# An attention, mixture-of-experts and FFN kernel: other places for sums, gates' steps and transposes, and a shifted buffer

## The chip, the cores and the metric

The kernel runs on one core of one Trainium2 chip. The metric is the time of one execution on the device, in microseconds (us). Before the change the median of three runs is 2119.26 us (2117.87 to 2119.72).

## The reference, cut to what matters

Three layers follow one another on 2304 tokens (4 x 576):

```python
# 1. attention with random features, 4 batches x 8 heads x 576 x 64, 128 features
q_p, k_p = phi(q_s), phi(k_s)               # exp(x @ omega.T - |x|^2/2 - max) / sqrt(m)
num = q_p @ (k_p.T @ v);  den = q_p @ k_p.sum(tokens) + 1e-6
x = (num / den)                             # -> [2304, 512]
# 2. eight experts, all of them for all tokens, D = 512, F = 1024
P = np.exp(x @ w_gate - max)
for _ in range(8):                          # the gates
    P /= P.sum(1, keepdims=True) + 1e-9
    P /= P.sum(0, keepdims=True) + 1e-9
    P *= N / E
out = sum(P[:, e:e+1] * (np.maximum(x @ w1[e], 0) @ w2[e]) for e in range(8))
# 3. FFN, d_ff = 2048
h = out @ w_in
return (h * sigmoid(1.702 * h)) @ w_out
```

## The kernel before

**Numbers in two parts.** Products on TensorE (PE) are made of three: an operand is split in a high part, rounded to `fp32r` by a cast on ACT, and a low part, the difference, made on DVE or POOL (`split`, L577). So a tile `w` gives `g0h`, `g0l` and so on, `x` gives `xh` and `xl`, and hh is followed by hl.

**Tiles.** The tokens lie in three blocks `j` of six tiles of 128. A weight chunk has 256 columns of `d_ff`: four chunks for each expert, eight for the FFN, which the code counts as expert 8 (`E`). A *visit* is one chunk on one block. It has an `up` part (x times w1, tiles `ph`) and a `down` part (h times w2, tiles `py`, 36 matmuls of 512 columns in 18 or 36 steps, `down`, L890 to L917), whose results are added into `acc` (`add_up`).

**Order of visits.** Expert 0's visits run between the pieces of the attention (half blocks, as soon as their x is there), the last of them behind it. Then come experts 1 to 7 and the FFN. In all these later visits but the FFN's first chunk, `up_fast` (L803 to L888) takes the place of `up`: seven products of six matmuls (le, ri, pc, le, ri, le, pd, L822) in place of eight, three of which have as their operand not x but sums of its quarters, the tiles `th` and `tl`. These sums are made once per block and layer, on POOL, DVE and ACT (`x_sums` L744, `x_sum4` L780, with the helpers `pool_tt` L735 and `dve_tt` L739). The first fast visit starts at 409.9 us.

**What sets the order.** The order is that in which the code is written: generators give work in pieces, and each `yield` gives the planned length of the PE work just issued (0.68 us for three `py`, 2.08 for twelve `ph`, 1.04 for a product of `up_fast`). At each yield the driver (L1113) makes one step of `background()` (L975), which issues the next sum of x, and at every third yield one step of `gates`. Every engine does its own instructions in the order of issue.

- `urgent` holds the sums of x in two lanes, `spare` the FFN's weights. `background()` issues from `urgent` whenever something is there; a fast visit that needs sums not yet issued takes them by `hurry`.
- `split1` (L631) splits a chunk's w1: three casts on ACT, then g0l, g1l and g2l on POOL. It is called in `down` of the visit before.
- `sinkhorn` (L478 to L521) makes the gates in turns of two steps. Step A is five DVE instructions (r, r, rr, lg, cs, L496 to L503). Step B is the PE product `pc` of ones and cs (L508) and three DVE instructions (ct, rc, lg, L511 to L513). There are eight turns.
- `ffn_in` (L1007) turns the FFN's x: for each tile four PE transposes (`xt`, L342), then the copy to yh and the difference yl. It runs beside the `down` parts of three visits about the end of expert 7; `late` holds subtractions that are put off.
- In `down`, `outer` chooses the order of the loops over the two halves `f` of w2 and the three tiles `t`: with `outer` f is the outer loop.

```python
        outer = cur.fast and e == E and not final          # L896
            if cnt % 3 == 2:                               # L1115
                next(gates, None)
            background()
```

Of the kernel before, what the change touches and what calls it, by code (L numbers as in the profile page):

```python
# [10 lines left out]
F32 = mybir.dt.float32  # L11
# [9 lines left out]
def tile_performer_sinkhorn_moe(  # L21
# [23 lines left out]
    E, _, F = w1.shape  # L45
    F2 = w_in.shape[1]
    P = 128
# [13 lines left out]
    ST = 6  # L61
    NB = NTILE // ST
# [5 lines left out]
    sm = ctx.enter_context(tc.tile_pool(name="sm", bufs=1))  # L68
# [21 lines left out]
    now = [0.0]  # L90
# [17 lines left out]
    def ps(name):  # L108
        return pp.tile([P, 512], F32, tag="ps", bufs=6, name=name)
# [13 lines left out]
    om_lo = ph["sb"].tile([P, 2 * M], F32R, name="om_lo")  # L123
    wg_raw = ph["sb"].tile([P, NK, E], F32, name="wg_raw")
    wg = ph["sb"].tile([P, NK, 2 * E], F32R, name="wg")
    lg = cst.tile([P, NTILE, E], F32, name="lg")
    pg = lg

# [59 lines left out]
    late = []  # L188

    def run_late():  # L190
        while late:
            late.pop(0)()
# [144 lines left out]
    def transpose_x(x, t, dst_h, dst_l):  # L337

        c = slice(t * P, (t + 1) * P)
        pt = ps("xt")  # L340
        for kk in range(NK):
            nc.tensor.transpose(pt[:, kk * P : (kk + 1) * P], x[:, kk * P : (kk + 1) * P], ident)  # L342
        pv = pt.rearrange("p (k n) -> p k n", k=NK)
        nc.scalar.copy(dst_h[:, :, c], pv)
        late.append(
            lambda: nc.vector.tensor_tensor(
                out=dst_l[:, :, c], in0=pv, in1=dst_h[:, :, c].bitcast(F32), op=ALU.subtract
            )
        )
# [301 lines left out]
    acc = {}  # L651
# [75 lines left out]
    sums_done = set()  # L727
# [162 lines left out]
    def down(cur, j, h, halves, first, final):  # L890

        e, _ = cur.ch
        if (e // E, j) not in accs:
            accs.add((e // E, j))
            acc[j] = new_acc(j, "a" if e < E else "o")
        outer = cur.fast and e == E and not final  # L896
        for th in halves:
            py = {}
            halves = range(NF) if th == 0 else range(NF - 1, -1, -1)
            tiles = range(3 * th, 3 * th + 3)  # L900
            todo = [(f, t) for f in halves for t in tiles] if outer else [(f, t) for t in tiles for f in halves]
            for f, t in todo:
                if t not in py:
                    py[t] = ps("py")
                c = slice(t % 3 * P, (t % 3 + 1) * P)
                hh, hl = h[th, f]
                w2h, w2l = cur.w2[f]
                for m, (a, w) in enumerate(((hh, w2h), (hh, w2l), (hl, w2h))):
                    nc.tensor.matmul(  # L909
                        py[t], a[:, c], w,  # L910
                        start=f == halves[0] and m == 0, stop=f == halves[1] and m == 2,
                    )
                if f == halves[1]:
                    add_up(cur, j, t, py[t], first, final)
                    if t > tiles[0]:
                        run_late()
                yield 3 * 0.2275  # L917
# [37 lines left out]
    n_exp = len(visits)  # L955
# [9 lines left out]
    urgent = [deque(), deque()]  # L965
    spare = deque()

    def run(q):
        if next(q[0], "end") == "end":
            q.popleft()  # L970
# [4 lines left out]
    def background():  # L975

        if begun():
            run(spare)
        elif any(urgent):
            for lane in urgent:  # L980
                if lane:
                    run(lane)
        elif spare and may_start[0]:
            run(spare)

    def hurry(q):

        force[0] = True
        run(spare if begun() else q)
        force[0] = False  # L990
# [3 lines left out]
            hurry(q)  # L994

    may_start = [False]

    def apply_gate(j):

        for _ in gates:  # L1000
            pass
        for t in range(ST):
            yield
            o = acc[j][:, t, :]
            nc.scalar.activation(o, o, AF.Copy, scale=pg[:, ST * j + t, 0:1])

    def ffn_in(j):  # L1007

        nblk[j] = hi, lo = new_block("y")
        for t in range(ST):  # L1010
            yield
            transpose_x(acc[j][:, t, :], t, hi, lo)
            yield
            run_late()

    nblk = {}

    def moe():

        cn = v = 0  # L1020
        for idx, (ch, j, halves) in enumerate(visits):
            if idx:
                new = ch != visits[idx - 1][0]
                cn, v = (cn + 1, 0) if new else (cn, v + 1)
            cur, nx, n2 = (chunks[cn + i] if cn + i < len(chunks) else None for i in range(3))
            left = 1
            while idx + left < len(visits) and visits[idx + left][0] == ch:
                left += 1
            while idx < n_first and not ready.issuperset((j, th) for th in halves):
                yield None  # L1030
            may_start[0] = cur.fast and ch[0] < E and left > 1
            if idx == n_exp - NB - 1:
                settle(spare)
            if n_exp <= idx < n_exp + NB:
                blk_h[j], blk_l[j] = nblk[j]

            def prep(at, cur=cur, v=v):
                if at == "w2" and v == 0:
                    if cur.fast:
                        cur.split2(len(cur.w2))  # L1040
                    else:
                        cur.split2(0)
                        cur.split2(1)

            key = (ch[0] // E, j)
            if cur.fast:
                for kk, lane in enumerate(urgent):
                    while (key, kk) not in sums_done:
                        hurry(lane)
                h = yield from up_fast(cur, j, prep)  # L1050
            else:
                h = yield from up(cur, j, halves, prep)
            if v == 0 and nx:
                nx.load2()
            if nx and left <= 2:
                nx.make_sums()
            side = None
            if n_exp - 2 <= idx <= n_exp:
                side = ffn_in(idx - n_exp + 2)
            elif n_first - 1 <= idx < n_first + 2:  # L1060
                side = apply_gate(idx - n_first + 1)
            first = (key, halves[0]) not in seen
            seen.update((key, th) for th in halves)
            for n, dt in enumerate(down(cur, j, h, halves, first, ch == chunks[-1].ch)):
                if n == 2 * len(halves) - 1 and left == 1 and nx:
                    for i in range(3):
                        nx.split1(i, nc.gpsimd)
                    if n2:
                        n2.load1()
                if side and (n > 4 or idx != n_first - 1):  # L1070
                    next(side, None)
                yield dt
            for _ in side or ():
                pass
            if idx == n_first - 1 or ch == (E, 0):
                sum_up(x_sum4(key, blk_h[j], blk_l[j]))
            if n_exp - 2 <= idx <= n_exp:
                i = idx - n_exp + 2
                sum_up(x_sums((1, i), *nblk[i]))

    with tc.manual_schedule():
        setup()
        load_tile("k", 0, NT)
        for what, t in (("v", 0), ("v", 1), ("q", 0), ("v", 2), ("q", 1), ("v", 3), ("v", NT), ("q", 2), ("q", 3)):
            load_tile(what, 0, t)
        load_gate()
        chunks[0].load1()
        chunks[0].load2()
        m = moe()
        credit = 0.0  # L1090
        for i, dt in enumerate(attention()):
            if i == 14:
                setup_gate()
            if i == 22:
                for g in range(3):
                    chunks[0].split1(g, nc.gpsimd)
                chunks[1].load1()
            credit += dt
            while credit > 0:
                got = next(m)  # L1100
                if got is None:
                    credit = 0.0
                else:
                    credit -= got
        enter_phase("exp")
        ready.update((j, th) for j in range(NB) for th in range(2))
        spare.extend(double_pieces())
        for j in range(NB):
            sum_up(x_sums((0, j), blk_h[j], blk_l[j]))
            if j < 2:  # L1110
                sum_up(x_sum4((0, j), blk_h[j], blk_l[j]))
        pool[0] = now[0]
        for cnt, dt in enumerate(m):  # L1113
            now[0] += dt
            if cnt % 3 == 2:  # L1115
                next(gates, None)
            background()
        phase.close()
# [30 lines left out]
```

## Time and profile before

| | us |
|---|---|
| median of three runs | 2119.26 |
| profiled execution, its own time | 2119.29 |
| its span in the trace | 2116.0 |
| PE busy | 2086.4 (99%) |
| DVE, ACT, POOL busy | 1419.0, 797.3, 500.7 |
| mean granted clock of the PE | 0.996 |

The span is 3.3 us shorter than the time of the execution it belongs to. PE is busy nearly always, by the table of busy time; since a matmul's end is modelled there, a wait is better read from the start times of the timeline, and a clock of less than 1 from the table of stretches (1 is 2.4 GHz, the lower level is 1.2 GHz). A row of a timeline has in brackets how long the engine sat idle before it and what released it.

### The profile page before, as it was taken

What the parts mean: (1) busy time and instruction counts of PE and PEld (TensorE: products, weight loads), DVE (VectorE), ACT (ScalarE), POOL (GpSimd) and SP (SyncE); (2) the same over time, 40 slices, a digit from 0 to 9 for tenths busy, and PEclk for the clock granted to TensorE, in tenths of its full rate; (3) what the DMA queues carried; (4) which work ended last, traced back from release to release, by engine and by line L of the source; (5) the groups of instructions that cost most, each with busy time, mean ns of one, the idle gap of its engine ahead of it and who ended that gap; (6) DMA issues with size and microseconds to landing.
All of it is one profiled execution on the core that took longest, in us unless ns stands there. A gap on an engine that the chain in (4) does not pass through costs nothing.

```text
span 2116.0 us, 29301 instructions
## 1 busy us (share of the span) xinstructions
PE 2086.4 (99%) x11040; PEld 1891.9 (89%) x11040; DVE 1419.0 (67%) x2630; ACT 797.3 (38%) x1770; POOL 500.7 (24%) x517
## 2 busy tenths in 40 slices
PE   8999998999999999999999999999999999999999
PEld 8999987899899998999989999899899988989987
DVE  7666546866767667676666676665555586676666
ACT  7655543433223232232333323223333255443443
POOL 3222225712212211121122111211211048111120
PEclk9999999999999999999999999999999999999999
DMA  8333211211111111111112111110010000000002
GB/s 164 89 81 90 70 41 40 65 43 43 50 45 43 51 60 43 50 50 43 46 43 58 53 50 43 51 38 21 22 39 21 20 21 21 21 21 21 21 21 90
DMA packets 147965, 100.54 MB, mean 48 GB/s; under 512 B 63600, under 2 KB 125040, under 8 KB 147824
## 3 DMA queue, kind: packets, MB, share of 16 engines
q1 hardware_dynamic: 147824, 98.68, 16.8%
q8 instruction: 86, 1.41, 0.3%
q14 instruction: 55, 0.45, 0.1%
HBM read 85.54 MB, written 13.11 MB: 47 GB/s over the span
## 4 chain that ended last, share of the span: by engine, by line
PE 94%; DVE 3%; ACT 2%; issue 0%; POOL 0%; DMA 0%; SPq 0%; ACTq 0%; POOLq 0%; DVEq 0%
PE py L909 45%; PE le L822 15%; PE ri L822 10%; PE ph L713 6%; PE pc L822 5%; PE pd L822 5%; PE num L304 2%; PE kv L274 1%; PE xt L342 1%; PE pt L215 1%; PE qt L297 1%; PE pj L240 1%; PE pj L242 1%; PE pj L241 1%; DVE mx L244 1%
## 5 line engine op out<-in xcount | busy, mean ns | idle before, releaser
L909 PE MATMUL py<-w,hh 128*128 128x512 f32 x2880 | 896.9, 392 | 1.8 <-ACT hh L676 1.8
L909 PEld LDWEIGHTS py<-w,hh 128*128 128x128 f32 x2880 | 534.0, 188 | 106.4 <-ACT hh L676 3.5
L909 PE MATMUL py<-w,hl 128*128 128x512 f32 x1440 | 564.2, 392 | 0.0
L926 DVE SCALAR_TENSOR_TENSOR a<-py,lg,a 128x512 f32<-128x512 f32 x504 | 367.1, 746 | 136.7 <-PE py L909 136.3
L909 PEld LDWEIGHTS py<-w,hl 128*128 128x128 f32 x1440 | 270.5, 188 | 59.1 <-DVE hl L684 1.7
L579 POOL TENSOR_TENSOR g0l<-w,g0h 128x768 fp32r<-128x768 f32 (+1 forms) x52 | 87.1, 1675 | 724.8 <-ACT g0h L578 706.2
L840 ACT COPY m<-le 128x384 f32<-128x384 f32 x105 | 50.3, 479 | 540.3 <-PE le L822 540.3
L563 POOL TENSOR_TENSOR tmp<-tmp 128x256 f32<-128x256 f32 x64 | 47.3, 738 | 637.3 <-DVE tmp L560 347.4
L833 DVE TENSOR_TENSOR pc<-pc,m 128x384 f32<-128x384 f32 x105 | 59.5, 566 | 147.1 <-PE pc L822 147.1
L628 POOL TENSOR_TENSOR w<-w 128x256 f32<-128x256 f32 x140 | 109.6, 804 | 44.8 <-DMA w<-scr_in 22.3
L579 DVE TENSOR_TENSOR w<-r,w 128x512 fp32r<-128x512 f32 x104 | 78.8, 771 | 52.3 <-ACT w L578 52.2
L578 ACT CAST w<-r 128x512 fp32r<-128x512 f32 x104 | 63.6, 629 | 116.1 <-PE py L909 115.5
L686 DVE SCALAR_TENSOR_TENSOR hl<-pc,hh 128x384 fp32r<-128x384 f32 x84 | 46.8, 557 | 90.1 <-ACT hh L678 88.4
L854 ACT COPY u<-le 128x384 f32<-128x384 f32 x105 | 50.5, 481 | 135.4 <-PE le L822 135.4
L260 ACT ACTIVATE feat<-pj,nb 128x128 f32<-128x128 f32 x272 | 74.0, 386 | 68.6 <-DVE nb L256 65.1
L930 DVE TENSOR_TENSOR o<-py,o 128x512 f32<-128x512 f32 x126 | 84.0, 685 | 21.7 <-PE py L909 21.7
L833 DVE TENSOR_TENSOR le<-le,m 128x384 f32<-128x384 f32 x105 | 59.3, 565 | 45.7 <-ACT m L874 45.7
L678 ACT ACTIVATE hh<-ri 128x384 fp32r<-128x384 f32 x84 | 41.2, 491 | 92.2 <-DVE ri L833 92.2
L822 PE MATMUL le<-th,g1h 128*128 128x384 f32 x210 | 71.5, 340 | 1.0 <-ACT m L840 1.0
L822 PE MATMUL le<-th,g2h 128*128 128x384 f32 x210 | 71.5, 340 | 0.9 <-ACT u L854 0.9
L874 ACT COPY m<-pd 128x384 f32<-128x384 f32 x105 | 49.9, 475 | 57.3 <-PE pd L822 57.2
L822 PE MATMUL ri<-th,g0h 128*128 128x384 f32 x210 | 71.4, 340 | 0.0
(253 smaller groups left out, 4599.8 us busy)
## 6 DMA issues: line engine op xcount, KB each, us to landing
w<-in_moe_w_dram SPq DMA_DIRECT2D x176, 128.0 KB, 2.3
r<-in_moe_w_dram SPq DMA_DIRECT2D x44, 512.0 KB, 3.7
raw<-in_moe_w_in_dram SPq DMA_DIRECT2D x32, 256.0 KB, 3.0
raw<-in_moe_w_out_dram SPq DMA_DIRECT2D x32, 256.0 KB, 3.0
k<-in_k_dram SPq DMA_DIRECT2D x16, 256.0 KB, 4.0
v<-in_v_dram SPq DMA_DIRECT2D x16, 256.0 KB, 4.8
q<-in_q_dram SPq DMA_DIRECT2D x16, 256.0 KB, 4.6
scr_in<-tmp SPq DMA_DIRECT2D x32, 128.0 KB, 1.9
```

What stands on the lines that cost most here:

```text
L260: nc.scalar.activation(f[:, h, :], pvs[h // 4][:, h % 4, :], AF.Exp, bias=nb[:, h : h + 1])
L578: nc.scalar.copy(hi, r)
L579: eng.tensor_tensor(out=lo, in0=r, in1=hi.bitcast(F32), op=ALU.subtract)
L628: nc.gpsimd.tensor_tensor(out=r[:, o], in0=r[:, x], in1=r[:, y], op=ALU.subtract)
L713: nc.tensor.matmul(o, w[kk][a], x[j][:, 2 * kh + kk, th * Q : (th + 1) * Q], start=m == 0, stop=m == 3 * NK - 1,)
L822: nc.tensor.matmul(o, a[kk][x], b[kk][y], start=start and kk == 0 and n == 0, stop=kk == 1 and n == 2, skip_group_check=True,)
L833: nc.vector.tensor_tensor(out=o, in0=a, in1=b, op=ALU.add)
L840: nc.scalar.copy(m1, le)
L854: nc.scalar.copy(u2, le)
L909: nc.tensor.matmul(py[t], a[:, c], w, start=f == halves[0] and m == 0, stop=f == halves[1] and m == 2,)
L926: nc.vector.scalar_tensor_tensor(out=o, in0=py, scalar=pg[:, n, e : e + 1], in1=o, op0=ALU.mult, op1=ALU.add)
L930: nc.vector.tensor_tensor(out=o, in0=py, in1=o, op=ALU.add)
```

## The change

1. A tile `pad` of 32 bytes per partition is put in the pool that lies ahead of others in the on-chip memory. `th` and `tl`, which began 32 bytes past a multiple of 64, begin on a multiple of 64; so do the tiles om_hi and om_lo of the attention. Some others (feat, ft, some of the temporaries) begin at 32 past it instead; x, h and the weights stay on 64.
2. While a `down` part of expert 0 runs behind the attention, `background()` issues no sum of x (if none of `spare` is begun), up to the point where the next chunk's splits are issued.
3. `gates` makes a step when 2.7 us of planned time have gone by since the last one, instead of at every third yield.
4. `ffn_in` issues the transposes of three tiles together, the first three tiles in the `up` part of the visit, the others in `down`.
5. In the FFN's last chunk `outer` holds too, but for the last half block.

```diff
+    sm.tile([P, 8], F32, name="pad")
...
-        outer = cur.fast and e == E and not final
         for th in halves:
+            outer = cur.fast and e == E and not (final and th == 1 and j == NB - 1)
...
         if begun():
             run(spare)
+        elif any(urgent) and paused[0]:
+            return
         elif any(urgent):
...
-        for t in range(ST):
-            yield
-            transpose_x(acc[j][:, t, :], t, hi, lo)
-            yield
-            run_late()
+        for g in range(0, ST, 3):
+            for t in range(g, g + 3):
+                transpose_x(acc[j][:, t, :], t, hi, lo)
+            for _ in range(3):
+                yield
+                if late:
+                    late.pop(0)()
+            for _ in range(3):
+                yield
...
+                if side and n > 0 and idx >= n_exp - 2:
+                    next(side, None)
...
+            paused[0] = ch[0] == 0
             for n, dt in enumerate(down(cur, j, h, halves, first, ch == chunks[-1].ch)):
                 if n == 2 * len(halves) - 1 and left == 1 and nx:
                     for i in range(3):
                         nx.split1(i, nc.gpsimd)
                     if n2:
                         n2.load1()
+                    paused[0] = False
...
+        gate_at = now[0]
         for cnt, dt in enumerate(m):
             now[0] += dt
-            if cnt % 3 == 2:
+            if now[0] > gate_at:
+                gate_at = now[0] + 2.7
                 next(gates, None)
```

Each engine has the same instructions as before; where they stand is shown at three places. Line numbers from 124 on are one higher in the changed kernel, and more further down.

**POOL, where the attention has ended** (one chunk of expert 0 gives way to the next at 311 to 320 us; u and t are temporaries of the sums, xh and xl the first block's x). Before:

```order
L735 TENSOR_TENSOR u<-xh,t 128x384
L735 TENSOR_TENSOR u<-u,xl 128x384
L735 TENSOR_TENSOR u<-xh,t 128x384
L735 TENSOR_TENSOR u<-u,xl 128x384
L579 TENSOR_TENSOR g0l<-w,g0h 128x2x256
L579 TENSOR_TENSOR g1l<-w,g1h 128x256
L579 TENSOR_TENSOR g2l<-w,g2h 128x256
```

After:

```order
L580 TENSOR_TENSOR g0l<-w,g0h 128x2x256
L580 TENSOR_TENSOR g1l<-w,g1h 128x256
L580 TENSOR_TENSOR g2l<-w,g2h 128x256
L736 TENSOR_TENSOR u<-xh,t 128x384
L736 TENSOR_TENSOR u<-u,xl 128x384
L736 TENSOR_TENSOR u<-xh,t 128x384
L736 TENSOR_TENSOR u<-u,xl 128x384
```

The three splits have come ahead of the first four sums.

**DVE, the third turn of the gates** (the end of step B of the second turn, step A, step B; tl is a sum of x, hl a low part of h). Before:

```order
L512 RECIPROCAL rc<-ct 128x8
L513 SCALAR_TENSOR_TENSOR lg<-lg,rc 128x144
L496 TENSOR_REDUCE r<-lg 128x18
L497 TENSOR_SCALAR r<-r 128x18
L498 RECIPROCAL rr<-r 128x18
L499 TENSOR_TENSOR lg<-lg,rr 128x144
L503 TENSOR_REDUCE cs<-lg 128x8
L511 TENSOR_SCALAR ct<-pc 128x8
L512 RECIPROCAL rc<-ct 128x8
L513 SCALAR_TENSOR_TENSOR lg<-lg,rc 128x144
L739 TENSOR_TENSOR xl<-u,xh 128x384
L739 TENSOR_TENSOR t<-xh,xl 128x384
```

After:

```order
L513 RECIPROCAL rc<-ct 128x8
L514 SCALAR_TENSOR_TENSOR lg<-lg,rc 128x144
L687 SCALAR_TENSOR_TENSOR hl<-ph,hh 128x384
L497 TENSOR_REDUCE r<-lg 128x18
L498 TENSOR_SCALAR r<-r 128x18
L499 RECIPROCAL rr<-r 128x18
L500 TENSOR_TENSOR lg<-lg,rr 128x144
L504 TENSOR_REDUCE cs<-lg 128x8
L740 TENSOR_TENSOR tl_3887<-u,th_3886 128x384 x2
L512 TENSOR_SCALAR ct<-pc 128x8
L513 RECIPROCAL rc<-ct 128x8
L514 SCALAR_TENSOR_TENSOR lg<-lg,rc 128x144
```

Step B of the third turn follows step A directly before; now there are two sums and, on PE, more matmuls between them.

**PE, the end of the last-but-one visit of expert 7's last chunk** (a is the first block's sum over the experts, turned for the FFN). Before:

```order
L822 MATMUL pd<-xl,g2h 128x384
L909 MATMUL py<-w_16288,hh 128x512
L909 MATMUL py<-w_16289,hh 128x512
L909 MATMUL py<-w_16288,hl 128x512
L909 MATMUL py<-w_16300,hh 128x512
L909 MATMUL py<-w_16301,hh 128x512
L909 MATMUL py<-w_16300,hl 128x512
L342 MATMUL xt<-ident,a_1111 128x128 x4
L909 MATMUL py<-w_16288,hh 128x512
```

After:

```order
L823 MATMUL pd<-xl,g2h 128x384
L910 MATMUL py<-w_16289,hh 128x512
L910 MATMUL py<-w_16290,hh 128x512
L910 MATMUL py<-w_16289,hl 128x512
L343 MATMUL xt<-ident,a_1112 128x128 x12
L910 MATMUL py<-w_16301,hh 128x512
L910 MATMUL py<-w_16302,hh 128x512
L910 MATMUL py<-w_16301,hl 128x512
```

Four transposes behind every six `py` have become twelve at a time; the other twelve of this block stand in the `up` part ahead, behind its second product.

## Rows read from the trace of the kernel before

**Rows 1.** the page's chain that ended last, shares of the span by engine

```profile
PE 94%; DVE 3%; ACT 2%; issue 0%; POOL 0%; DMA 0%; SPq 0%; ACTq 0%; POOLq 0%; DVEq 0%
```

**Rows 2.** stretches: length, busy us (xcount) PE, PEld, DVE, ACT, POOL, clock, DMA

```profile
313.00:327.00 14.00, 9.12 (x35) 8.14 (x33) 5.29 (x7) 1.86 (x4) 6.57 (x7) 0.76 0.25 77
342.00:354.00 12.00, 9.63 (x38) 7.64 (x37) 10.97 (x21) 4.66 (x10) 9.70 (x10) 0.86 0.00 0
```

**Rows 3.** waits, 300 to 426 us: engine, line, releaser; total us, times, longest

```profile
PE pc L508 <- DVE cs L503: 7.9, 4, 2.4
PE ph L713 <- POOL g2l L579: 4.9, 1, 4.9
PE le L822 <- ACT m L840: 1.0, 1, 1.0
```

**Rows 4.** timeline: start, us, engine, line, op, tiles [idle before]

```profile
311.44 0.41 ACT L578 CAST g2h<-w 128x256 fp32r<-128x256 f32 x1
...
311.86 1.26 POOL L735 TENSOR_TENSOR u<-xh,t 128x384 f32<-128x384 f32 x1 [10.99 <-DVE t L739]
...
319.79 0.69 PE L713 MATMUL ph<-xh,g2l 128*128 128x384 f32 x1 [4.88 <-POOL g2l L579]
...
325.96 0.34 PE L713 MATMUL ph<-xl,g0h 128*128 128x384 f32 x1
```

**Rows 5.** timeline of POOL near 370 us: one split by itself

```profile
370.30 0.73 POOL L579 TENSOR_TENSOR g2l<-w,g2h 128x256 fp32r<-128x256 f32 x1
```

**Rows 6.** timeline of DVE: first and last instruction of two steps A

```profile
347.22 0.30 DVE L496 TENSOR_REDUCE r<-lg 128x18 f32<-128x144 f32 x1
349.31 0.41 DVE L503 TENSOR_REDUCE cs<-lg 128x8 f32<-128x144 f32 x1
...
370.43 0.29 DVE L496 TENSOR_REDUCE r<-lg 128x18 f32<-128x144 f32 x1
371.74 0.43 DVE L503 TENSOR_REDUCE cs<-lg 128x8 f32<-128x144 f32 x1
```

**Rows 7.** groups by forms (busy, mean ns), then PE's timeline of a visit

```profile
L822 PE MATMUL le<-th,g1h 128*128 128x384 f32 x210 | 71.5, 340 | 1.0 <-ACT m L840 1.0
L822 PE MATMUL le<-xh,g0h 128*128 128x384 f32 x168 | 57.1, 340 | 0.0
L822 PE MATMUL pc<-xh,g0h 128*128 128x384 f32 x168 | 56.4, 336 | 0.0
...
1800.93 0.34 PE L822 MATMUL le<-th,g1h 128*128 128x384 f32 x1
...
1801.99 0.34 PE L822 MATMUL ri<-yh,g1h 128*128 128x384 f32 x1
...
1803.04 0.34 PE L822 MATMUL le<-th,g2h 128*128 128x384 f32 x1
...
1804.10 0.34 PE L822 MATMUL pd<-yh,g2h 128*128 128x384 f32 x1
...
1805.14 0.63 PE L909 MATMUL py<-w,hh 128*128 128x512 f32 x2
...
1813.34 0.33 PE L822 MATMUL le<-yh,g0h 128*128 128x384 f32 x1
```

**Rows 8.** timeline of PE and POOL where the FFN begins

```profile
1715.46 0.63 PE L909 MATMUL py<-w,hh 128*128 128x512 f32 x2
...
1725.44 1.29 POOL L579 TENSOR_TENSOR g0l<-w,g0h 128x512 fp32r<-128x512 f32 x1
...
1726.42 0.42 PE L713 MATMUL ph<-yh,g0h 128*128 128x384 f32 x1
```

**Rows 9.** POOL's tile u (min/median/max ns), and the end of expert 1's splits

```profile
L735 POOL TENSOR_TENSOR u<-u,xl x18: 992/1015/1347, 313.2 to 419.5; 128x384 f32<-128x384 f32 x18
...
411.58 1.62 POOL L579 TENSOR_TENSOR g2l<-w,g2h 128x512 fp32r<-128x512 f32 x1
```

**Rows 10.** timeline of PE in the last chunk, the first block

```profile
2071.17 0.73 PE L909 MATMUL py<-w,hh 128*128 128x512 f32 x2 [0.20 <-ACT hh L676]
```

More of the change, by code (lines that the diff above doesn't have):

```diff
@@ L996, in tile_performer_sinkhorn_moe @@
     may_start = [False]
+    paused = [False]
     def apply_gate(j):
@@ L1045, in moe @@
             key = (ch[0] // E, j)
[L1046 to L1056, printed above, removed]
             side = None
@@ L1061, in moe @@
                 side = apply_gate(idx - n_first + 1)
+            if cur.fast:
+                for kk, lane in enumerate(urgent):
+                    while (key, kk) not in sums_done:
+                        hurry(lane)
+                todo = up_fast(cur, j, prep)
+            else:
+                todo = up(cur, j, halves, prep)
+            n = 0
+            while True:
+                try:
+                    dt = next(todo)
+                except StopIteration as end:
+                    h = end.value
+                    break
+                if side and n > 0 and idx >= n_exp - 2:
+                    next(side, None)
+                n += 1
+                yield dt
+            if v == 0 and nx:
+                nx.load2()
+            if nx and left <= 2:
+                nx.make_sums()
             first = (key, halves[0]) not in seen
             seen.update((key, th) for th in halves)
+            paused[0] = ch[0] == 0
             for n, dt in enumerate(down(cur, j, h, halves, first, ch == chunks[-1].ch)):
```

## The prediction

> **What bounds the kernel now.** I read the page first: the chain that ended last runs through TensorE (PE) for 94% of the span [rows 1], so the time is the PE's own stream plus the moments in which it waits or runs at half its clock. Then the table of stretches, to see where those moments are: between 313 and 354 us the granted clock falls to 0.76 and 0.86 while PE is busy for only 9 to 10 us out of 12 to 14 [rows 2]. The table of waits from 300 to 426 us names the causes: one wait for the last weight split of expert 0 on POOL, four waits of `pc` for the gates' column sums on DVE, one for a copy on ACT [rows 3]. The timelines then give each wait its place. Everything ahead of 250 us and from 426 to 1710 us is a PE stream without such holes; there only the length of a matmul itself could change.
>
> The changed kernel issues the same instructions on every engine in another order, so the sum is made of waits that go or come, of half clock behind them, and of matmuls that may get shorter. It is made against the profiled execution's 2119.29 us, which is the median of the runs (2119.26) to 0.03 us; the 3.3 us around the span stay.
>
> **1. Weight splits ahead of the sums.** The three casts that feed the splits are over at 311.85, but POOL has just begun four sums (u at 311.86, about 1.1 us each), and the splits come behind them; PE, which had asked at about 314.9, gets g2l only at 319.79 and has waited 4.88 [rows 4]. In the new order (shown with the change) the splits stand ahead of those four sums. Alone, the three take 1.29 + 0.73 + 0.73 = 2.75 us [rows 5, 8], since g1l has g2l's shape; begun behind the first cast, two casts of 0.4 earlier at about 311.1, they are done between 313.9 and PE's asking at 314.9. Gain 4.9, bounds 4.0 (splits stretched as beside DVE work) and 5.3.
>
> Behind that wait the PE ran at half its clock: from 319.79 to 325.96 it started 19 matmuls in 6.17 us [rows 4], where a group of six takes 1.05 at full clock [rows 7], so 19 take 3.33. Lost: 2.8, which goes with the wait; 0 if something else still lets the clock fall there.
>
> **2. Gates' steps by time.** The four waits of `pc` cost 7.9 us on the PE's row [rows 3], 8.5 with the matmuls that restart behind them. Each step A (five DVE instructions, from r to cs) is followed by step B, whose `pc` needs cs. Before, B follows A by three yields, which are three pieces of 0.68 us (2.05) wherever both fall in `down`; now by at least 2.7 by the kernel's own count, so at least 0.68 more for each of the four: 2.7. Step A itself takes 2.09 + 0.4 = 2.5 beside POOL's sums and 1.31 + 0.4 = 1.7 with POOL at rest [rows 6], and POOL's sums now pause in each `down` of expert 0 until the splits are out: up to 0.8 more each, 3.1. Gain between 2.7 and 5.8; I take the middle, 4.3, since the pause covers part of those stretches only; the outer bound is all 8.5. What stays is hidden by nothing: the PE waits in order, with all later `py` behind it. The wait at 347 to 350 us was followed by a clock of 0.86 over 12 us [rows 2], 12 x 0.14 = 1.7 lost. I count 1.7, bounds 0 and 1.7.
>
> **3. The sums that are put off.** The PE's 1.0 us wait for a copy in the first fast visit [rows 3] lies beside a crowded ACT, POOL and DVE; with the gates' end shifted I take that gain as 1.2. In exchange about 22 sums of x and four weight sums (3.5) stand behind expert 1's splits, which end at 413.2 [rows 9]. A fast visit takes 7 x 1.05 + 8.2 = 15.6 [rows 7]; the last product on sums in expert 1's third visit comes 2 x 15.6 + 5 x 1.05 = 36.4 behind the start of its first (409.9), and 33 of these are left when the splits end. At 1.02 each (median) they need 22 x 1.02 + 3.5 = 25.9, at 1.35 each (the longest) 33.2 [rows 9]; with the ACT casts and DVE subtractions between them that comes near what is there. Cost 0.8, bounds 0 and 4.5 (1.35 each, and about 4 us of chained casts that POOL waits for). Net gain 0.4, bounds +1.2 and -3.3.
>
> **4. Transposes in two groups.** Now six groups of four stand between the `py` of one block: 1715.46 to 1726.42, 10.96 us, where 36 `py` alone take 8.20 (1805.14 to 1813.34) [rows 7, 8]. That is 0.46 per group of four, nearly all of it the four transposes' own time, which stays; fewer turns give 0 to 0.3. But half of each block's transposes leave for `up`, so the PE comes to (E,0)'s first `ph` at 8.20 + 3 x 0.46 = 9.6 us behind its first `py`, while POOL, with sums of the FFN's x ahead of it, ends g0l at 1725.44 + 1.29 - 1715.46 = 11.3 [rows 8]. The second matmul of `ph` needs g0l: a new wait of 1.4 (PE asks 0.3 later), bounds 0.2 (if the sums move up with the transposes that feed them) and 2.5, with 1.7 of half clock behind it at worst. The pause doesn't help here, it holds for expert 0 alone. Net -1.1 (slower), taken as +1.4 less 0.3.
>
> **5. Last chunk by w2 halves.** In the last chunk the second `py` pair of each block waits 0.20 for the second half of h, and that pair takes 0.73 [rows 10] where 0.63 is usual [rows 7]: 0.3 for each of three blocks, 0.9. In the new order the first half's matmuls of three tiles come first, 2.0 us of cover rather than 0.68. A tile's output then closes later, but the last half block keeps its order. Bounds 0 and 1.7.
>
> **6. Sums of x on 64 bytes.** The new tile of 32 bytes moves th and tl from 32 past a multiple of 64 bytes onto it. In one visit, two groups of six matmuls on th take 1.06 each (1800.93, 1803.04) and the two behind them on yh take 1.05 and 1.04 [rows 7]: 0.015 a group. Three groups in each of 105 visits (210 matmuls of each form, two in a visit) make 315 x 0.015 = 4.7. By the durations alone, 340 against 336 ns [rows 7], 18 x 105 x 4 ns would be 7.6; nothing at all is the other end. The features and the second layer's temporaries go to 32 past instead; none of them is a moving operand of 384 columns, and I count 0 for them, bounds 0 and +1.
>
> The Trainium skill ("TensorE: Matmul & The Clock Gate", section "Wait — 56ns, not 53.3ns?") gives the start-to-start time as the columns over 2.4 GHz plus about 2.5 ns, here 162.5, whatever the address. The rows show 1.05/6 = 175 and 1.06/6 = 177, so the case is above that rule for both, and differs between operands, which the rule has no room for. By the rule part 6 would be 0 and the sum 2105.4.
>
> **Sum.** 2119.3 - 4.9 - 2.8 - 4.3 - 1.7 - 0.4 + 1.1 - 0.9 - 4.7 = **2100.7 us**.
>
> **The rivals.** *R1, the address is not what makes th slow.* The groups on th would then stay at 1.06 and the time be 2100.7 + 4.7 = 2105.4. For it: the first group of a visit, le on xh, which is on 64 bytes already, also shows 340 ns [rows 7]. Against it: th is slow in all three places, behind different neighbours, with one pattern. The rule above would also end here, with the same 2105.4.
> *R2, new waits eat more.* The wait at (E,0) becomes 2.5 with 1.7 of half clock behind it (+2.8 over my 1.4), and the third visit of expert 1 waits 4.5 instead of 0.8 (+3.7): 2107.2. For it: POOL's queue is in order, and both places have sums ahead of what the PE needs. Against it: before, sums behind a queue like that kept up [rows 9].
> *R1 and R2 together*: 2111.9.
> *R3, slower.* The paused sums themselves become the path. They would have to end some 23 us behind expert 1's third visit: 3.5 + 22 m = 33 + 23, m = 2.4 us for each. The longest here is 1.35 [rows 9], so POOL would have to be held by DVE nearly all of the time. Then 2122 or more.
> *R4, all goes right*: the four waits vanish wholly (-4.2), the third visit is in time (-0.8) and no new wait comes at (E,0) (-1.4): 2094.3.
>
> **How the numbers follow.** Forecast 0.56, R1 0.22, R2 0.10, both 0.04, R4 0.05, R3 0.03. Cases are uncertain by 2 us on either side, so the range goes from R4 to a little above R2: 2094 to 2109; what lies outside is R3, both rivals together and the tails, under 2 in 10. A measurement of this kernel can tell about 0.2% (4.2 us) from no change: faster means below 2115.0. All but R3, and a part of both together, is far below it: faster 0.95, same 0.02, slower 0.03.
>
> **What would show it.** Part 1: no PE wait for g2l near 315 us and no clock below 1 up to 327. Part 2: the `pc` waits sum to about 4 instead of 7.9, the clock stays full at 350. Part 3: the waits list of expert 1's third visit names sums (tl, xl, POOL) for under 1 us. Part 4: one PE wait on g0l at the first `ph` of the FFN of 1 to 2 us. Part 5: no wait of `py` for hh in the last chunk. Part 6: the six matmuls on th take 1.045 to 1.05, and le, ri on th have 336 ns in the table by forms; if they keep 340, R1 holds. Wrong would be a time above 2109, from a new wait that this list doesn't name, or below 2094, from matmuls that get shorter elsewhere too.

## The result and the profile after

The changed kernel takes 2096.89 us (median of 4 runs, 2095.94 to 2099.11) where the kernel before takes 2118.57; the ratio is 0.9901, with a 95% interval from 0.9884 to 0.9919. That is 21.7 us less, where 18.6 had been forecast (2100.7, range 2094 to 2109). The profiled execution took 2097.55 us with a span of 2095.7, against a span of 2116.0 before: 20.3 us less. The other 1.5 us of the profiled pair lie outside the span (3.3 before, 1.8 now), and that part varies by itself: 26 executions of the kernel before spread from 1.8 to 3.0.

First the page of the changed kernel: the busy time of the engines, and the chain that ended last by engine (as [rows 1]).

```profile
PE 2075.8 (99%) x11040; PEld 1883.2 (90%) x11040; DVE 1415.8 (68%) x2630; ACT 796.9 (38%) x1770; POOL 502.1 (24%) x517
...
PE 93%; DVE 3%; ACT 2%; POOL 1%; issue 1%; DMA 0%; SPq 0%; ACTq 0%; POOLq 0%; DVEq 0%
```

PE is the bound as before, with 10.6 us less of busy time (2086.4 before); the rest of the 20.3 was idle time of PE. The next rows are the table of stretches (length, busy us of PE, PEld, DVE, ACT, POOL, then the granted clock), which answer to [rows 2].

```profile
313.00:327.00 14.00, 14.00 (x71) 11.80 (x69) 11.50 (x24) 3.78 (x8) 6.42 (x6) 1.00 0.26 77
342.00:354.00 12.00, 12.00 (x66) 11.06 (x65) 9.52 (x22) 6.16 (x15) 8.29 (x8) 1.00 0.24 67
354.00:375.00 21.00, 19.39 (x99) 16.93 (x98) 18.24 (x41) 5.36 (x12) 12.84 (x14) 1.00 0.19 62
```

The clock is 1.00 in all three, and in the first two PE is busy throughout, where it was busy for 9.12 of 14 and 9.63 of 12 us. PE's waits from 300 to 440 us (total, times, longest), which answer to [rows 3]:

```profile
PE pc L509 <- DVE cs L504: 1.6, 2, 1.1
PE le L823 <- ACT m L841: 1.1, 1, 1.1
```

The wait for g2l is gone. Two waits for cs are left of four, 1.6 us of 7.9. A wait for a copy on ACT is there again, now in expert 1's third visit instead of its first. The place of [rows 4] on POOL and PE:

```profile
311.33 1.29 POOL L580 TENSOR_TENSOR g0l<-w,g0h 128x512 fp32r<-128x512 f32 x1 [10.49 <-ACT g0h L579]
312.58 1.05 POOL L580 TENSOR_TENSOR g1l<-w,g1h 128x256 fp32r<-128x256 f32 x1
313.59 1.06 POOL L580 TENSOR_TENSOR g2l<-w,g2h 128x256 fp32r<-128x256 f32 x1
314.61 1.03 POOL L736 TENSOR_TENSOR u<-xh,t 128x384 f32<-128x384 f32 x1
...
314.79 0.37 PE L714 MATMUL ph<-xh,g2l 128*128 128x384 f32 x1
```

The splits run from 311.33 to 314.65, in front of the sums, and PE's matmul on g2l starts at 314.79 with no wait. The groups by forms, in answer to [rows 7] (busy us, mean ns):

```profile
L823 PE MATMUL le<-th,g1h 128*128 128x384 f32 x210 | 70.2, 334 | 1.3 <-ACT m L841 1.1
L823 PE MATMUL le<-xh,g0h 128*128 128x384 f32 x168 | 57.0, 340 | 0.0
L823 PE MATMUL pc<-xh,g0l 128*128 128x384 f32 x168 | 56.8, 338 | 0.0
```

Matmuls on th have 334 ns instead of 340; those on x stay about where they were. Last, what is new: PE's waits where the FFN begins, 1690 to 1810 us.

```profile
PE ph L714 <- POOL g0l L580: 1.9, 1, 1.9
PE py L910 <- ACT hh L677: 1.2, 1, 1.2
PE le L823 <- ACT u L855: 1.0, 1, 1.0
PE xt L343 <- DVE hl L685: 0.6, 1, 0.6
```

The 1.2 and 1.0 us for ACT were there before, too. The 1.9 for g0l and the 0.6 of a transpose are new.

### The profile page after: what moved, and what is told of

Its sections match the earlier page's. It is cut to its first block, busy times and chain, and to the rows that moved or that the text cites. A ratio compares the mean times of both kernels' runs of the same rounds, so it can differ in the third digit from the quotient of the medians.

```text
span 2095.7 us, 29308 instructions
## 1 busy us (share of the span) xinstructions
PE 2075.8 (99%) x11040; PEld 1883.2 (90%) x11040; DVE 1415.8 (68%) x2630; ACT 796.9 (38%) x1770; POOL 502.1 (24%) x517
## 4 chain that ended last, share of the span: by engine, by line
PE 93%; DVE 3%; ACT 2%; POOL 1%; issue 1%; DMA 0%; SPq 0%; ACTq 0%; POOLq 0%; DVEq 0%
PE py L910 45%; PE le L823 15%; PE ri L823 10%; PE ph L714 6%; PE pc L823 5%; PE pd L823 5%; PE num L305 2%; PE kv L275 1%; PE qt L298 1%; PE pj L241 1%; PE pt L216 1%; PE pj L242 1%; PE xt L343 1%; PE pj L243 1%; DVE mx L245 0%
## 5 line engine op out<-in xcount | busy, mean ns | idle before, releaser
L687 DVE SCALAR_TENSOR_TENSOR hl<-pc,hh 128x384 fp32r<-128x384 f32 x84 | 46.8, 558 | 85.3 <-ACT hh L679 84.0
L823 PE MATMUL ri<-tl,g0h 128*128 128x384 f32 x210 | 70.4, 335 | 0.0
```

Of the source, the lines that this page charges most:

```text
L823: nc.tensor.matmul(o, a[kk][x], b[kk][y], start=start and kk == 0 and n == 0, stop=kk == 1 and n == 2, skip_group_check=True,)
```

## The experiments

Each kernel is compared with the kernel before on the same chip, in three sets of runs. In the first (pad32, pad64, pause, gates) the kernel before took 2114.36 us, in the second (pad96, pause_gates, old_xt, pause_ffn) 2118.83, in the third (shift64, xt_pad96, xt_pad96_g34) 2116.92. These medians differ by as much as some of the effects, mostly through the clock (see the last section), so small differences between ratios of different sets say little; the parts are read from the traces. Where a time of a visit stands, it is the sum over its 42 matmuls in `up_fast` of the median start-to-start time over 105 visits.

**The address alone.** Three kernels have the order of before and only a tile of another size ahead of th and tl:

```diff
     wg = ph["sb"].tile([P, NK, 2 * E], F32R, name="wg")
+    sm.tile([P, 8], F32, name="pad")        # pad32; 16 in pad64, 24 in pad96
```

> The kernel before with nothing but the 32-byte tile ahead of th and tl, so that both begin on a multiple of 64 bytes; the order of all work is that of before. My theory (the address makes th's matmuls slow): each group of six on th falls from 1.060 us to about 1.035, the x group behind it may rise a little; 63 ns in each of 105 visits, 6.6 us in all, as the changed kernel's trace shows: time 2112 to 2113, waits and clock as before. Rival (th's groups got shorter because the other edits moved work of other engines away from them): groups on th stay at 1.060 us, time 2119 as before.

> The kernel before with a tile of 64 bytes in the same place: th and tl move by 64 bytes and still begin 32 past a multiple of 64. My theory: nothing changes, groups on th stay at 1.060 us, time 2119 (within 2). Rival (any shift against the neighbouring tiles does it): the groups fall to about 1.035 us here too and the time is 2112 to 2113.

> The kernel before with a tile of 96 bytes: th and tl begin on a multiple of 64 that is not one of 128 (as x, y and w2 do). Theory A (64 bytes are what counts): the same as with 32 bytes, groups on th near 1.034 us, a visit 63 ns shorter than before, about -6. Theory B (the place against other tiles counts, since 64 bytes of shift already took 39 ns off a visit): another value again, between 0 and 39 ns off a visit, groups on th of 1.04 to 1.06.

Ratios: 0.9974 (0.9963 to 0.9985) with 32 bytes, 0.9988 (0.9978 to 0.9998) with 64, 0.9942 (0.9927 to 0.9957) with 96. Forms with 32 bytes, with 64 and with 96 bytes, one on th and one on x each:

```profile
L823 PE MATMUL le<-th,g1h 128*128 128x384 f32 x210 | 70.0, 334 | 1.0 <-ACT m L841 1.0
L823 PE MATMUL pc<-xh,g0l 128*128 128x384 f32 x168 | 56.8, 338 | 0.0
```

```profile
L823 PE MATMUL le<-th,g1h 128*128 128x384 f32 x210 | 70.5, 336 | 1.0 <-ACT m L841 1.0
L823 PE MATMUL pc<-xh,g0l 128*128 128x384 f32 x168 | 56.4, 336 | 0.0
```

```profile
L823 PE MATMUL le<-th,g1h 128*128 128x384 f32 x210 | 70.3, 335 | 1.0 <-ACT m L841 1.0
L823 PE MATMUL pc<-xh,g0l 128*128 128x384 f32 x168 | 56.1, 334 | 0.0
```

The means hide the pattern, which the start-to-start times show (ns, one group on th, then the group on x behind it):

```
before  (th 96 past a multiple of 128)  176 178 174 179 174 179   177 174 175 173 173 173   visit 7381
pad64   (32 past)                       170 174 176 177 178 175   174 174 175 173 173 173   visit 7342
pad32   (0 past; changed kernel too)    169 173 173 173 173 173   176 182 173 173 173 173   visit 7319
pad96   (64 past, as x)                 173 173 173 173 173 173   173 173 173 173 173 173   visit 7295
```

So the address is the cause: the order of before with 32 bytes has the changed kernel's pattern. But "a multiple of 64" isn't the whole of it. With 64 bytes th still lies 32 past a multiple of 64, and 39 of the 62 ns come all the same; with 32 bytes a price is left in the first two matmuls that go from th to x; with 96 bytes, where th lies as x does, nothing is left: 86 ns a visit, 9.0 us in 105. From the first fast visit's start to the last matmul the traces are 6.0 (32), 4.1 (64) and 8.1 us (96) shorter than before.

> The kernel before with 64 bytes ahead of all weights, x, y and h and a tile of 96 bytes ahead of th and tl: everything that the fast visits multiply begins on a multiple of 128, th and x still at the same distance from it, where in the run with 96 bytes all of it lies 64 past a multiple of 128. Theory A (th must lie as x does): the same as with 96 bytes, all seven groups but the first at 173 ns a matmul, a visit 87 ns shorter than before, time 2105. Theory B (64 past a multiple of 128 is by itself the good place, 0 the lesser one): the groups on th and x show the 169, 176 and 182 ns of the run with 32 bytes, or the py change from 227 ns, time 2107 or more.

```diff
+    sm.tile([P, 24], F32, name="pad")
     lg = cst.tile([P, NTILE, E], F32, name="lg")
+    cst.tile([P, 16], F32, name="pad0")     # 64 bytes ahead of w, g, x, y, h, w2
```

```profile
L824 PE MATMUL le<-th,g1h 128*128 128x384 f32 x210 | 70.3, 335 | 1.0 <-ACT m L842 1.0
L824 PE MATMUL pc<-xh,g0l 128*128 128x384 f32 x168 | 56.1, 334 | 0.0
```

These are the rows of the run with 96 bytes again, and a visit takes 7.295 us, as there, though everything lies on a multiple of 128 now. In these runs it is the place of th relative to the other operands that counts, not the multiple. (Whether it is relative to x or to the weights can't be told: these lie alike in all runs.) From the first fast visit's start to the last matmul the trace is 8.2 us shorter than before, also as with 96 bytes, and `py` is unchanged, at 227 ns. The ratio, 0.9967 (0.9955 to 0.9979), shows less of a gain than with 96 bytes; its trace has three stretches at half the clock ahead of 353 us, the run with 96 bytes has one; see the clock below.

**The pause and the gates' steps, each alone and together.**

```diff
# pause
+        elif any(urgent) and paused[0]:
+            return
...
+            paused[0] = ch[0] == 0
...
+                    paused[0] = False
# gates
+        gate_at = now[0]
...
-            if cnt % 3 == 2:
+            if now[0] > gate_at:
+                gate_at = now[0] + 2.7
```

> The kernel before with the pause of the sums alone (gates' steps at every third yield as before). My theory (the splits' place in POOL's queue sets PE's wait at 315 us): the 4.9 us wait for g2l and the 2.8 us of half clock behind it go, the four waits for cs stay within 1.5 us of their 7.9, with half clock behind one of them: -6 to -8, time 2111 to 2113. Rival (POOL's sums also make step A long, so that the pause alone removes most of the waits of pc): these fall below 4 us too, -10 or more, time below 2109.

> The kernel before with the gates' steps by time alone. My theory: the wait for g2l at 315 us and the half clock behind it stay (4.9 + 2.8), the waits for cs fall from 7.9 to 2 to 4 us, and no half clock follows them: -5 to -7.5, time 2112 to 2114. Rival (the steps' distance does little while POOL's sums run beside step A): waits for cs stay above 5, time 2115 or more.

> The kernel before with the pause and the gates' steps by time, no other edit. Theory A (the two work only together: each alone left 5 us of waits for cs): waits for cs of 1.6 us as in the changed kernel, none for g2l, no half clock between 310 and 410: about -13, time 2101 beside 2114. Theory B (the gates' steps add nothing to the pause, as they changed nothing alone): -8, as the pause alone, with about 5 us of waits for cs.

PE's waits from 300 to 440 us with the pause alone, with the gates' steps alone, and with both:

```profile
PE pc L508 <- DVE cs L503: 5.2, 2, 3.2
PE le L822 <- ACT m L840: 1.0, 1, 1.0
```

```profile
PE ph L713 <- POOL g2l L579: 5.1, 1, 5.1
PE pc L508 <- DVE cs L503: 4.9, 5, 1.8
...
PE le L822 <- POOL g0l L579: 0.9, 1, 0.9
```

```profile
PE pc L508 <- DVE cs L503: 1.6, 2, 1.1
PE le L822 <- ACT m L840: 1.1, 1, 1.1
```

The pause alone gives 0.9962 (0.9949 to 0.9975): the wait for g2l goes, as forecast, and of the waits for cs two of four go with it, but one of the two that stay is longer (3.2 where 2.4 was the longest). Neither theory has it whole: 5.2 is above the rival's 4 and below the 6.4 of mine. The gates' steps alone give nothing in the time, 0.9998 (0.9989 to 1.0008), and there my theory fell: the waits for cs fall from 7.9 to 4.9 us only (8.5 to 5.7 from start to start), the wait for g2l is 5.1, and a new one for g0l in the first fast visit takes 0.9 back. The 1.0 us for ACT's copy stays, too, and half clock follows one more wait (0.88 over 372 to 386 us). Its rival, that the distance does little while the sums run beside step A, is nearer. Together they give 0.9928 (0.9913 to 0.9943), and waits for cs of 1.6: 6.3 us of them gone, where each alone took 2.7 and 3.0.

What the two share is the length of step A. Two steps of the changed kernel, one with POOL idle and one beside the splits (first and last instruction on DVE; for the second, POOL's first split):

```profile
348.93 0.29 DVE L497 TENSOR_REDUCE r<-lg 128x18 f32<-128x144 f32 x1
350.11 0.45 DVE L504 TENSOR_REDUCE cs<-lg 128x8 f32<-128x144 f32 x1
...
369.69 1.67 POOL L580 TENSOR_TENSOR g0l<-w,g0h 128x512 fp32r<-128x512 f32 x1 [2.62 <-ACT g0h L579]
370.13 0.30 DVE L497 TENSOR_REDUCE r<-lg 128x18 f32<-128x144 f32 x1
372.24 0.41 DVE L504 TENSOR_REDUCE cs<-lg 128x8 f32<-128x144 f32 x1
```

The first takes 1.6 us, the second 2.5. In the traces of before, of these three runs and of the changed kernel a step with POOL idle takes 1.6, and every wait for cs in the table of waits stands behind a step of 2.0 us or more that ran beside work of POOL. Before, six of eight steps are that long; in the changed kernel five have POOL idle, and the two that PE still waits for ran beside the splits, which the pause does not move away from step A.

**The transposes.**

```diff
# old_xt: the changed kernel with
-        for g in range(0, ST, 3):
...
+        for t in range(ST):
+            yield
+            transpose_x(acc[j][:, t, :], t, hi, lo)
+            yield
+            run_late()
...
-                if side and n > 0 and idx >= n_exp - 2:
+                if False:
# pause_ffn: the changed kernel with
-            paused[0] = ch[0] == 0
+            paused[0] = ch[0] == 0 or idx == n_exp - 1
```

> The changed kernel with the last layer's transposes as they were before (four at a time, all in the down parts). Theory A (the two groups cost more than they save, through the wait for g0l): the 1.9 us wait for g0l at the FFN's first product falls to 0.2 to 0.5 and the 0.6 us wait of a transpose goes, -2 to -3 against the changed kernel, time 1 to 3 us less. Theory B (the regrouping pays for its wait elsewhere): the stretch from expert 7's last chunk to the FFN's second chunk is as long as in the changed kernel or longer, time the same within 1 or more.

> The changed kernel with the pause of the sums also in the down part that comes ahead of the FFN's first chunk, so that its splits go ahead of the sums of y on POOL. Theory A (the wait for g0l is made by the sums ahead of it): g0l ends about 4 us earlier, the 1.9 us wait goes, -2.1 against the changed kernel; the sums put off are not missed, since their first use is 50 us later. Theory B (the split waits for its cast on ACT, or the sums put off come late at the FFN's second chunk): the wait stays over 1 us, or one as long comes at the second chunk: 0 to -0.5.

With the old transposes the ratio is 0.9888 (0.9872 to 0.9905), 2093.61 us, where the changed kernel took 2096.89 in other runs. The intervals of the two ratios overlap, so the trace has to show that it is faster. PE's waits from 1690 to 1810 us:

```profile
PE py L910 <- ACT hh L677: 1.2, 1, 1.2
PE le L823 <- ACT u L855: 1.0, 1, 1.0
```

Both new waits are gone. From the start of the first fast visit to the first product of the FFN's second chunk it takes 1364.3 us, the changed kernel 1366.9: the regrouping cost 2.6 us, as much as its waits. The wait for g0l in the changed kernel, in answer to [rows 8] (timeline of POOL, then of PE):

```profile
1705.44 1.01 POOL L736 TENSOR_TENSOR u<-u,yl 128x384 f32<-128x384 f32 x1
1706.40 1.59 POOL L580 TENSOR_TENSOR g0l<-w,g0h 128x512 fp32r<-128x512 f32 x1
...
1708.04 0.44 PE L714 MATMUL ph<-yh,g0l 128*128 128x384 f32 x1 [1.94 <-POOL g0l L580]
```

The last sum of the FFN's x ends at 1706.45 and g0l starts behind it, as forecast. Yet taking the sums away from there did not help: with the longer pause the ratio is 0.9917 (0.9903 to 0.9932), 2099.43 us. g0l starts at 1700.08 there, and PE's waits from 1700 to 1810 us are

```profile
1700.08 1.30 POOL L580 TENSOR_TENSOR g0l<-w,g0h 128x512 fp32r<-128x512 f32 x1 [6.63 <-ACT g0h L579]
```

```profile
PE py L910 <- DVE hl L685: 4.3, 3, 2.0
PE xt L343 <- ACT o L925: 0.9, 1, 0.9
PE py L910 <- ACT hh L677: 0.6, 1, 0.6
```

The wait for g0l is gone, and 4.3 us for low parts of h on DVE came in its place, over the same and the following visits, where the sums that had been put off now run on DVE and ACT between the steps that make hl (that they are the cause is read from the timeline, no run tests it). Theory A was right on the cause of the wait, and wrong that the sums wouldn't be missed.

**The last chunk.**

```diff
-            outer = cur.fast and e == E and not (final and th == 1 and j == NB - 1)
+            outer = cur.fast and e == E and not final      # old_last
```

> The changed kernel with the last chunk's loops as they were before (tiles outside, halves of w2 inside). Theory A (that edit is worth the three waits for h): PE waits three times 0.2 us for hh in the last chunk, 0.37 to 0.43 from start to start each, and the stretch from the last chunk's first product to the end is 1.1 to 1.3 us longer than in the changed kernel. Theory B (the reordered loops only close their outputs later, the end comes no sooner): the stretch is as long as in the changed kernel, within 0.2 us.

```profile
PE py L910 <- ACT hh L677: 0.7, 3, 0.2
```

The three waits of [rows 10] are back (the row is PE's in the table of waits, 2030 to 2094 us; the changed kernel has none there), 0.41 us each from start to start. The stretch from the last chunk's first product to the last matmul is 48.3 us against 46.8: 1.6 longer, of which the waits are 1.2; the rest is matmuls that start behind them, 0.34 us apart instead of 0.23. One execution has no interval; the waits themselves are clear.

**What the runs point to.** The changed kernel with the old transposes and 96 in place of 32 bytes:

> The changed kernel with the old transposes and with a tile of 96 in place of 32 bytes. If the two edits add up: a visit takes 7.295 in place of 7.318 us in its up part, 105 x 0.023 = 2.4 us less than with the old transposes alone, time 2091 to 2092, waits as there. If the address gain belongs to the order of the kernel before only: 2093.6 as there.

> The same with 3.4 in place of 2.7 us between the gates' steps. Theory A (the distance of the steps is what the two last waits for cs lack): the 1.6 us of waits for cs (1.9 from start to start) fall below 0.5, -1.4 or more: 2089.5 to 2090.5. Theory B (the last steps now come late for expert 0's last block, which is scaled by the gates): the waits go, but PE waits at the first fast visits for copies on ACT, over 1.3 us as now: no gain, or up to 2 us lost.

The first gives 2090.47 us (2090.17 to 2090.7), ratio 0.9883 (0.9869 to 0.9898): it beats both kernels. The changed one took 6.4 us more, in other runs and with overlapping intervals of the ratios; from the first fast visit's start to the last matmul the traces differ by 4.7 us, 2.7 for the transposes and 2.1 for the shift (2.4 forecast), so the two edits add up. With 3.4 us between the gates' steps it is 2092.82, ratio 0.9897 (0.9878 to 0.9915): no gain. PE's waits from 300 to 440 us in that one:

```profile
PE pc L509 <- DVE cs L504: 2.6, 2, 1.9
PE le L823 <- ACT m L841: 1.7, 2, 1.1
```

More distance made the waits for cs longer, 2.6 instead of 1.6 us, and a wait of 0.5 us in the first fast visit came back. The steps had moved beside other sums: the one at 370 us has three sums on POOL beside it and takes 2.6 us. Theory B's waits on ACT are there, but the waits for cs did not go, so neither theory was right.

## Why the prediction was right, and where it was not

The time, the sign and the range held, though not every term did: parts 2 and 6 gave 2.3 and 1.3 us more than forecast and part 4 cost 1.5 more, so the sum came closer than its terms. Point by point, in PE time from start to start:

1. *Splits ahead of the sums*: forecast 4.9 and 2.8 of half clock. Measured 5.0 of wait (another 0.3 in the first matmul behind it is within the half clock's 2.8), and the clock is 1.00 there. The run with the pause alone shows that this edit does it.
2. *Gates' steps*: forecast 4.3 of 8.5, measured 6.6 (1.9 left). This term was mis-sized. I gave the distance at least 2.7 us by itself and took 1.6 more for the pause. The runs show 2.8 for the distance alone, as reckoned, but also 3.0 for the pause alone, so the pause, which I had as the lesser part, is worth as much, and the whole is a little more than the sum. My short step A "with POOL at rest" was misread, too: g2l ran beside its first 0.6 us [rows 5, 6]; with POOL idle a step takes 1.6. Of the half clock behind the wait at 350 us (forecast 1.7) see below.
3. *Sums put off*: forecast a net gain of 0.4, with 0.8 lost in expert 1's third visit. Measured 1.2 gained in the first visit (1.46 to 0.28 from start to start) and 1.3 lost in the third: 0.1 lost. What I had as sums that come late is there a queue on ACT (ACT's rows, then PE's):

```profile
429.43 0.51 ACT L793 CAST xh<-u 128x384 fp32r<-128x384 f32 x1 [3.49 <-POOL u L736]
429.84 0.47 ACT L841 COPY m<-le 128x384 f32<-128x384 f32 x1
...
430.37 0.44 PE L823 MATMUL le<-th,g1h 128*128 128x384 f32 x1 [1.15 <-ACT m L841]
```

ACT stood for a cast whose sum on POOL was late; the copy that PE needs was behind it in ACT's queue. The sums themselves were in time.
4. *Transposes*: forecast 1.1 lost, measured 2.6. The wait that I named came, and old_xt shows that the regrouping makes it; the wait for g0l is 2.1 from start to start where I had 1.4, and 0.2 of it was there before. What I left out is the transposes in (E,0)'s `down`: there one of them waited 0.7 for DVE's hl, the last to read a `ph` tile. xt, ph and py share six PSUM buffers, so I take it that none was free; that is argued, not tested. That twelve together save 0 to 0.3 is not contradicted by the runs: 2.6 lost is what the two waits cost.
5. *Last chunk*: forecast 0.9, measured 1.4: the stretch from the last chunk's first product to the last matmul goes from 48.4 to 46.8 us, and 0.2 of that is part 6. The run that undoes the edit alone shows 1.6.
6. *Sums on 64 bytes*: forecast 4.7, with 7.6 as the most; measured 62 ns a visit, 6.5, and 6.0 from end to end in the run with 32 bytes. The sign and the bound held. The step that failed is the model: I compared th with the x groups behind it and took x as what an operand on 64 bytes does. In truth th lost more than that (1.060 to 1.034) and the x groups rose (1.045 to 1.050), so a group's time depends on its neighbour's address, too; 32 bytes are not the best shift, 96 are.

With 5.0, 6.6, -0.1, -2.6, 1.4 and 6.0 the sum is 16.3. Half clock gives another 4.5: three stretches ahead of 354 us before, which lost 1.7, 2.8 and 1.7, and one at 38 us after, which lost 1.7. The first of the three (0.57 over 291.5 to 295.5 us) and the one at 38 us (0.66 over 37 to 42) were in no forecast; the run with 32 bytes, in the order of before, has neither, so they are chance, and they cancel. That is 20.8 for the 20.3 by which the span is shorter. From the first fast visit's start on, parts 3 to 6 make 4.7, and so do the traces; the 0.5 too much lies ahead of it, and I have not settled it. That the kernel before was profiled with so much half clock helped the forecast: its executions elsewhere take as little as 2112.9 us, 6.4 less than the value forecast from (see the last section).

R1 fell with the first experiment. The rule that I had set beside part 6 (the Trainium skill, "TensorE: Matmul & The Clock Gate", section "Wait — 56ns, not 53.3ns?") leaves the address out; here matmuls of one size take from 169 to 185 ns, 173 where all lies alike, and the address alone moves them. Of R2, the wait at (E,0) came, without half clock behind it, and the third visit's wait stayed near my value. R3 did not come: the sums were late for ACT's queue, not for PE's operands.

## What to carry to other kernels

An edit that shows nothing in the time can still take waits away: the gates' steps alone took 3.0 us of waits for cs, while by their trace 0.9 of another wait and half clock behind one more took part of it back; beside the pause, which takes POOL's sums from the same chain, the gain showed. So read the waits, and not the time alone, before an edit is dropped. Work put off to clear one wait comes back where its own chain crosses a queue of another engine, so a wait that has been located is not yet one that can be removed (the longer pause cleared 1.9 us and made 4.3). And when one operand of a stream shows another time per matmul than its neighbour of the same shape, compare their start addresses and try more than one shift.

## What the runs showed of the hardware that was not expected

**Relative addresses.** 384-column matmuls took 173 ns from start to start when th lay like x relative to a multiple of 128 bytes (both 64 past, or both 0 past), 170 to 179 when it began 32 bytes off x's place, to either side, and, when the two lay 64 bytes apart, 169 at the change from x to th and 176 and 182 at the change from th to x. The first group of each visit, behind `py`, took 171 to 185 ns in every run, whatever the address; that stays unexplained.

**The clock.** The same order of work was followed by different amounts of half clock. Before, the clock was 0.76 behind the 5.0 us wait and 0.86 behind the wait at 347 us [rows 2]. The runs with 32 and with 64 bytes have the same order and the same waits; their stretches (length, busy us by engine, granted clock) are, with 32 bytes and then with 64,

```profile
311.00:325.00 14.00, 9.11 (x39) 7.98 (x38) 6.12 (x9) 2.22 (x4) 6.97 (x7) 0.88 0.25 77
341.00:353.00 12.00, 9.64 (x48) 8.21 (x47) 11.11 (x20) 6.11 (x13) 10.57 (x11) 1.00 0.11 31
```

```profile
311.00:325.00 14.00, 9.12 (x34) 8.06 (x34) 6.99 (x11) 2.29 (x5) 7.72 (x7) 0.76 0.27 77
341.00:353.00 12.00, 9.64 (x46) 7.84 (x46) 11.18 (x21) 5.57 (x12) 9.45 (x9) 1.00 0.00 0
360.00:372.00 12.00, 10.03 (x40) 8.11 (x39) 9.49 (x22) 2.95 (x7) 8.09 (x8) 0.86 0.17 46
```

With 32 bytes the clock is 0.88 behind the 5.0 us wait, and full behind the one of 2.5; with 64 bytes it is 0.76, full at that one, and 0.86 at the next, of 2.1 us (and 0.83 over 383 to 393 us, about the fourth). So the terms of 2.8 and 1.7 for half clock (1.2 GHz instead of 2.4) in the sum were those of one execution: behind the 5.0 us wait it came in all six traces that have this wait, with a clock of 0.76 or 0.88 over 14 us, behind shorter ones in some executions and at other places. The spread of the kernel before goes with it: in the first set its executions with a mean clock of 0.998 or 0.999 took 2112.9 to 2114.6 us, those with 0.996 or less 2117.2 to 2120.0. It is part of why ratios differ a little between kernels whose traces tell the same.
